# GELU by tanh from the exponential's table, its cubic on VectorE, and other shares of the score tiles

## The chip, the core and the metric

The kernel runs on one core of a Trainium2 chip. A core has TensorE (PE, matrix multiplies into the eight banks of PSUM), ScalarE (ACT, table functions), VectorE (DVE, elementwise work), GpSimd (POOL, a slower elementwise engine that has no part in PSUM here) and SyncE (SP, which issues transfers). They run side by side and wait for one another on semaphores. The metric is device time in microseconds: the median before is 809.54 over four runs (808.48 to 812.94).

## The reference

One transformer block over 2048 tokens of width 640, in bfloat16: a layer norm, attention with 32 query heads of width 20 that share one key and one value head, a residual, a second layer norm, a gated feed-forward with 1536 hidden columns, and a residual.

```python
h  = x + softmax(q @ k.T * 20**-0.5) @ v @ wo        # x normed first; 32 heads, one k and v
h2 = h + (gelu(n @ w_gate) * (n @ w_up)) @ w_down    # n = layernorm(h); gelu(approximate=True)
```

The GELU is the tanh form: 0.5 g (1 + tanh(0.79788 (g + 0.044715 g³))). The attention has 32 x 2048 x 2048 scores, and each of them needs an exponential.

## The kernel before, in words

**Packs.** The scores are made in packs. A unit is 512 query columns for four rows of the array; a pack is one key tile (128 keys) against a unit: four matmuls (L1037, "QK") that fill four PSUM banks, one score tile of 128x512 each. There are 512 packs, 64 for each pair of token tiles. Banks 0 to 5 hold scores, so a new pack needs four of six free: the two spare ones and two that the pack before must have given back. Banks 6 and 7 hold the sums of probabilities times values (L1116, "PV") and all other matmuls.

**Who makes the exponentials.** Of the four tiles of a pack some go to ScalarE, which takes one tile (128x512) or two neighbouring banks at once (128x1024) through `Exp` (L1375), and n go to VectorE, which makes an approximate exponential with a multiply and an add into a 16 bit integer (L1438, "d" below). Each such tile needs two shifted copies, one integer add each; GpSimd makes nearly all of them (L1416, 128x256 int32), VectorE now and then several at once (L1410). So a VectorE tile gives three PV matmuls, a ScalarE tile one. The usual pack has n = 1: one single and one pair for ScalarE, one d for VectorE, two adds for GpSimd.

**The order is planned at build time.** Each engine runs a fixed list. A planner walks simulated time with a cost for each instruction and picks, engine by engine, what to put next; the engines on the chip then follow these lists in order and wait on semaphores. `issue_qk` (L982) chooses n from the ScalarE backlog A and the VectorE load Dv: 0 where Dv is over `TH0`, otherwise 1, and in a burst (A over 3000 ns) 4 or 2. `act_decide` puts a ready ScalarE task ahead of the next exponential.

**The feed-forward.** It goes by batches: seven of two token tiles, and the last two tiles by themselves. Once both normed tiles of a batch stand in `xn2T`, `gate_job` makes the gate product in pieces of 512 columns (two hidden tiles of 128 by 256 tokens), and `up_job` the up product; `down_job` sums 12 matmuls for each half of a token tile. While there are exponentials left, a gate piece is copied from PSUM to `gbuf` by VectorE (L799), and when all six pieces of a batch are there, `gelu` runs `Gelu_apprx_tanh` over them in two ScalarE instructions of 1536 columns (L819). ScalarE holds one set of function tables; `Exp` and this GELU stand in different sets, so a table load (`ACT_TABLE_LOAD`) comes before the two and another after them. Then VectorE multiplies with the up product straight from PSUM (L836). After the last exponential, gates go from PSUM through GELU directly (L801).

Of the kernel before, what the change touches and what calls it, by code (L numbers as in the profile page):

```python
# [178 lines left out]
class _Job:  # L179


    __slots__ = ("name", "prio", "pieces", "bank", "then", "seq", "pos", "gate")

    def __init__(self, name, prio, pieces, then, gate=None):
        self.name = name
        self.prio = prio
        self.pieces = pieces
        self.then = then
        self.bank = None
        self.pos = 0  # L190
        self.gate = gate


def bass_sequential_preLN__grouped_kv_mqa__glu_gated_geglu__prompt_kernel(
# [39 lines left out]
    NQ = 4  # L234
    NXT = 4
    NON = 8

    allocs = []

# [5 lines left out]

    xh = sb("xh", [P, NT, D], BF16)
    xn1T = sb("xn1T", [P, NC_D, S], BF16)
    xn2T = sb("xn2T", [P, NC_D, 1024], BF16)
    wq_pad = sb("wq_pad", [P, NG, NC_D, P], BF16)
    wk_sb = sb("wk_sb", [P, NC_D, Dh], BF16)  # L250
    wk4 = sb("wk4", [P, NC_D, P], BF16)
# [12 lines left out]
    onq = sb("onq", [P, NON, D], BF16)  # L264
    onT = sb("onT", [P, 4, NC_D, P], BF16)
    gbuf = sb("gbuf", [P, NFC, 512], BF16)
    ident = sb("ident", [P, P], BF16)
    halfc = sb("halfc", [P, 4], BF16)
    warm = sb("warm", [P, 4], BF16)
# [40 lines left out]
    def c_dve(n):  # L310
        return n / 0.96 + 67.0

    POOL_ADD = 635.0
    ADD_MIN = 1
    PVF = 99
# [2 lines left out]
    PADD_LEN = 2  # L318
    PRA = 3
    PRD = 3  # L320
    TH0 = 1500.0
    TH2 = 0.0
    PAIR2 = 0
    ADDW = 50.0
    MISCMAX = 1500.0
# [38 lines left out]
    sp_tasks = []  # L364
    state = {"mode": "m", "tab": "exp", "npack": 0, "exps_left": 2048, "misc_ready": False, "kv_left": NT, "qk_left": 512}
    bank_owner = {b: None for b in range(8)}
    slots = {"xt": list(range(NXT)), "q": list(range(NQ)), "onT": list(range(4)), "osb": [0, 1], "rcp": [0, 1]}
    pa_free = [True] * NA
    pd_free = [True] * ND
    pd_next = [0]  # L370
# [23 lines left out]
    def ln_group(ln, tiles, prio, done):  # L394
        n = len(tiles)
        sl = slice(tiles[0], tiles[-1] + 1)
        cnt = [0]
        kk = (ln, tiles[0])

        def after_stats(op):  # L400
            cnt[0] += 1
            if cnt[0] == n:
                dve(lambda e: e.tensor_copy(ln_vb[:, ln, sl], mv[:, ln, sl, 1]), 80,
                    [("mv", ln, t) for t in tiles], [("vb", kk)], prio, c2)

        def c2(op):
            dve(lambda e: e.tensor_scalar_add(ln_veb[:, ln, sl], ln_vb[:, ln, sl], EPS), 80,  # L407
                [("vb", kk)], [("veb", kk)], prio, c3)

        def c3(op):  # L410
            task(("pool",), lambda e: e.tensor_tensor(ln_denb[:, ln, sl], ln_veb[:, ln, sl], halfc[:, 0:n], ALU.pow),  # L411
                 1010, L_POOL, [("veb", kk), "halfc"], [("den", kk)], prio, c4)

        def c4(op):
            dve(lambda e: e.reciprocal(ln_r[:, ln, sl], ln_denb[:, ln, sl]), 90, [("den", kk)], [("lr", kk)],
                prio, c5)

        def c5(op):
            for t in tiles:
                norm(t)  # L420

        def norm(t):
            slot = []

            def gate():
                return bool(slots["xt"])

            def start():
                slot.append(slots["xt"].pop(0))
                return slot[0]  # L430

            def then(op):
                s = slot[0]

                def tdone(op2):
                    slots["xt"].append(s)
                    done(t, op2)

                if ln == 0:
                    o = xn1T[:, :, t * P:(t + 1) * P]  # L440
                    wkeys = [("xn1T", t)]
                else:
                    o = xn2T[:, :, xcol[t]:xcol[t] + P]
                    wkeys = [("xn2T", xcol[t])]
                def free():
                    return ln == 0 or batch_of[t] < 2 or up_left[batch_of[t] - 2] == 0

                if t in (PE_T1 if ln == 0 else PE_T2):
                    tr_job(("tr", ln, t), xn_tmp[:, s, :], ("xt", s), o, wkeys, lambda: slots["xt"].append(s),
                           lambda op2: done(t, op2))  # L450
                    return
                sp_tasks.append(_Task(("sp",), lambda e: e.dma_start_transpose(o, xn_tmp[:, s, :]), 1330, 1700,
                                      [("xt", s)], wkeys, prio, tdone, free))

            keys = [("x", t)] if ln == 0 else [("h", t, 0), ("h", t, 1)]
            tk = _Task(("dve",), None, 310, L_DVE, keys + [("lr", kk)], [], prio, then, gate)

            def bind():
                s = start()
                tk.fn = lambda e: e.tensor_scalar(xn_tmp[:, s, :], xh[:, t, :], mv[:, ln, t, 0:1],  # L460
                                                  ln_r[:, ln, t:t + 1], ALU.subtract, ALU.mult)
                tk.writes = [("xt", s)]

            tk.born = bind
            tasks.append(tk)

        return after_stats
# [13 lines left out]
    xcol = {}  # L481
    for b, tl in enumerate(BATCHES):
        for i, t in enumerate(tl):
            xcol[t] = (b % 2) * 512 + i * P


    def free_bank(b):
# [235 lines left out]
    batch_of = {t: b for b, tl in enumerate(BATCHES) for t in tl}  # L723
    batch_x = [0] * len(BATCHES)
    down_left = [2 * len(tl) for tl in BATCHES]
    gate_left = [NFC] * len(BATCHES)
    up_left = [NFC] * len(BATCHES)
    copied = [[] for _ in BATCHES]

    def x2_done(t, op):  # L730
        b = batch_of[t]
# [40 lines left out]
    def bview(bk, b, k):  # L772
# [2 lines left out]
            return bank(bk, n)  # L775
        return bank(bk, n * k).rearrange("p (k n) -> p k n", k=k)

    def gate_job(b, fc):
        n = len(BATCHES[b]) * P
        k = per_job(b)  # L780
        ks = [x for i in range(k) for x in gkeys(b, fc + i)]

        def then(bk):
            def fin(op):
                free_bank(bk)
                gate_left[b] -= k
                copied[b].append(fc)
                if gate_left[b] == 0:
                    gelu(b)

            def fin2(op):
                free_bank(bk)
                gate_left[b] -= k
                up_job(b, fc)
                if gate_left[b] == 0 and copied[b]:
                    gelu(b)
            o, i = gview(b, fc, k), bview(bk, b, k)
            if state["exps_left"] > 0:
                dve(lambda e: e.tensor_copy(o, i), c_dve(n * k), [("b", bk)], ks, 1.0, fin)  # L799
            else:  # L800
                task(("act",), lambda e: e.activation(o, i, ACT.Gelu_apprx_tanh), ("gelu", c_act(n * k)), L_ACT,  # L801
                     [("b", bk)], ks, 1.0, fin2)
        jobs.append(_Job(("gate", b, fc), 5.0, gu_pieces(wg_sb, b, fc), then, lambda: g_free(b)))

    def gelu(b):
        k = per_job(b)
        fcs = sorted(copied[b])
        runs = []
        n = len(BATCHES[b]) * P
        most = max(k, 1536 // n)  # L810
        for fc in fcs:
            if runs and runs[-1][1] == fc and fc + k - runs[-1][0] <= most:
                runs[-1][1] = fc + k
            else:
                runs.append([fc, fc + k])
        for f0, f1 in runs:
            v = gview(b, f0, f1 - f0)
            ks = [x for fc in range(f0, f1) for x in gkeys(b, fc)]
            task(("act",), (lambda v: lambda e: e.activation(v, v, ACT.Gelu_apprx_tanh))(v),  # L819
                 ("gelu", c_act(n * (f1 - f0))), L_ACT, ks, ks, 1.0,  # L820
                 (lambda f0, f1: lambda op: [up_job(b, fc) for fc in range(f0, f1, k)])(f0, f1))

    def up_job(b, fc):
        n = len(BATCHES[b]) * P
        k = per_job(b)
        ks = [x for i in range(k) for x in gkeys(b, fc + i)]

        def then(bk):
            def fin(op):
                free_bank(bk)  # L830
                up_left[b] -= k
                if up_left[b] == 0:
                    for t in BATCHES[b]:
                        down_job(b, t, 0)
            o, i = gview(b, fc, k), bview(bk, b, k)
            dve(lambda e: e.tensor_tensor(o, i, o, ALU.mult), c_dve(n * k), [("b", bk)] + ks, ks, 1.0, fin)  # L836
        jobs.append(_Job(("up", b, fc), 4.0, gu_pieces(wu_sb, b, fc), then))

    def down_job(b, t, h):
# [142 lines left out]
    def issue_qk(t, u, kt, fb):  # L982
        A = max(act_end() - t, 0.0)
        Dv = dve_load(t)
        if state["tab"] == "gelu" or any(tk.engs[0] == "act" for tk in tasks):
            A += sum(tk.cost[1] for tk in tasks if tk.engs[0] == "act" and isinstance(tk.cost, tuple)) + 1300.0
        nf = pd_free.count(True) - len(dve_q)
        burst = A > 3000.0
        if state["npack"] < 4:
            n = 0  # L990
        elif burst:
            n = 4 if Dv < 2500.0 else 2
        elif Dv > TH0:
            n = 0
        elif Dv < TH2:
            n = 2
        else:
            n = 1
# [303 lines left out]
    def issue_piece(t, jb, pc):  # L1302
        if isinstance(jb, _Start):
# [3 lines left out]
            active.append(jb)  # L1307
            jb.bank = b
            bank_owner[b] = jb.name
            if jb.name[0] == "q":  # L1310
                units[jb.name[1]]["q"] = slots["q"].pop(0)
        b = jb.bank
# [335 lines left out]
```

## Time and profile before

| what | value |
|---|---|
| median of the runs | 809.54 us |
| profiled execution, time and span | 812.94 us and 811.1 us |
| granted TensorE clock, mean | 0.989 |
| ScalarE busy | 761.8 us, 94% of the span |
| TensorE, VectorE, GpSimd busy | 694.7, 571.2, 639.2 us |
| exponentials on ScalarE | 504 pairs, 505 singles; on VectorE 535 tiles |
| table loads | 16, of 1283 ns |
| copies of gates, products with up | 42 of 691 ns (L799), 48 of 683 ns (L836) |
| GpSimd's adds | 1036 of 616 ns |

The profiled execution is 3.4 us above the median, of which 1.8 us lie outside the span. Busy times are unions: neighbouring instructions of an engine overlap in the records, so a mean duration is longer than the step from one to the next. "Idle before" names what ended the idle time in front of a group; an engine that is not the bottleneck idles at no cost.

### The profile page before, as it was taken

The page shows a single profiled execution, that of the slowest core. Times are in us where ns is not written, and L with a number is a line of the kernel's source. Part 1 is how long each engine was busy: PE and PEld are TensorE (multiplying, and loading weights), DVE is VectorE, ACT ScalarE, POOL GpSimd, SP SyncE. Part 2 cuts the span into 40 slices and gives each one's busy share as a digit, 9 for nine tenths or more (in the row PEclk, how much of TensorE's full clock was granted, in tenths as well). Part 3 has the DMA queues.
Part 4 walks back from the last instruction along what each step waited for, and adds up shares of the span by engine and source line. Part 5 has one row for each costly group of instructions (what it writes and reads, how often), then busy time and mean ns, then how long its engine had stood idle before and what let it go on. Part 6 is the DMA issues. An engine that isn't in the chain of part 4 may idle for free.

```text
span 811.1 us, 30789 instructions
## 1 busy us (share of the span) xinstructions
PE 694.7 (86%) x13435; PEld 335.3 (41%) x13435; DVE 571.2 (70%) x1060; ACT 761.8 (94%) x1054; POOL 639.2 (79%) x1096
## 2 busy tenths in 40 slices
PE   4787778889789897889978898898988899888998
PEld 3432223444334443345434443354433444344457
DVE  7865557776687666776677766876668766777854
ACT  3699999999999999999999999999999999999991
POOL 5488788888888888888888888888888778888860
PEclk9899999999999999999999999999999989999999
DMA  7590000100020000000000000100000000000000
GB/s 205 82 336 2 2 1 18 20 2 13 22 21 3 2 19 19 19 2 3 18 19 19 2 11 19 26 3 2 19 18 19 2 2 19 19 18 11 11 19 18
DMA packets 40293, 22.01 MB, mean 27 GB/s; under 512 B 31328, under 2 KB 38880, under 8 KB 40160
## 3 DMA queue, kind: packets, MB, share of 16 engines
q1 hardware_dynamic: 37536, 19.18, 9.8%
q8 instruction: 107, 1.75, 0.9%
q10 hardware_dynamic: 2624, 0.87, 0.5%
q14 instruction: 26, 0.21, 0.1%
HBM read 10.21 MB, written 2.62 MB: 16 GB/s over the span
## 4 chain that ended last, share of the span: by engine, by line
ACT 80%; PE 12%; DVE 4%; DMA 2%; issue 1%; POOL 0%; ACTq 0%
ACT pa L1375 76%; PE ps L1037 3%; PE ps L498 3%; PE ps L1116 3%; PE ps L494 3%; ACT gbuf L819 2%; DVE pd L1438 2%; DMA gbuf<-in_A_wq_dram 1%; ACT L1375 1%; ACT L819 1%; DVE osb L1143 1%; DMA xn1T<-xn_tmp 1%; DVE xn_tmp L460 0%; DVE stats L391 0%; PE ps L1240 0%
## 5 line engine op out<-in xcount | busy, mean ns | idle before, releaser
L1375 ACT ACTIVATE pa<-ps 128x512 bf16<-128x512 f32 (+1 forms) x1009 | 713.2, 953 | 19.3 <-PE ps L1037 19.2
L1416 POOL TENSOR_TENSOR pd<-pd,shifts 128x256 int32<-128x256 int32 x1036 | 615.1, 616 | 130.2 <-DVE pd L1438 119.4
L1438 DVE TENSOR_SCALAR pd<-ps 128x512 uint16<-128x512 f32 x535 | 365.9, 690 | 208.1 <-PE ps L1037 201.8
L1116 PE MATMUL ps<-pd,v_ext 128*32 128x512 bf16 x1605 | 273.1, 385 | 32.7 <-DVE osb L1143 18.3
L1116 PE MATMUL ps<-pa,v_ext 128*32 128x512 bf16 x1513 | 265.4, 387 | 3.8 <-DVE pd L1438 1.7
L1037 PE MATMUL ps<-qT,kT 32*128 32x512 bf16 x2048 | 204.5, 385 | 60.6 <-DVE pd L1438 25.0
L1037 PEld LDWEIGHTS ps<-qT,kT 32*128 32x128 bf16 x2048 | 61.0, 91 | 218.3 <-DVE pd L1438 145.2
L1116 PEld LDWEIGHTS ps<-pd,v_ext 128*32 128x32 bf16 x1605 | 73.6, 95 | 93.1 <-ACT pa L1375 32.7
L1116 PEld LDWEIGHTS ps<-pa,v_ext 128*32 128x32 bf16 x1513 | 70.0, 95 | 48.1 <-issue 33.0
L498 PE MATMUL ps<-xn2T,wu_sb 128*32 128x256 bf16 x1680 | 62.3, 280 | 2.4 <-DVE gbuf L836 2.4
L498 PE MATMUL ps<-wd_sb,gbuf 128*32 128x320 bf16 x1344 | 64.1, 301 | 0.0
L498 PE MATMUL ps<-xn2T,wg_sb 128*32 128x256 bf16 (+1 forms) x1748 | 63.4, 272 | 0.7
L498 PEld LDWEIGHTS ps<-xn2T,wg_sb 128*32 128x32 bf16 x1748 | 42.1, 96 | 19.7 <-issue 12.2
L498 PEld LDWEIGHTS ps<-xn2T,wu_sb 128*32 128x32 bf16 x1680 | 42.4, 98 | 17.9 <-issue 9.5
L498 PE MATMUL ps<-xn1T,wq_pad 128*32 128x256 bf16 (+1 forms) x1440 | 48.0, 266 | 0.0
L498 PEld LDWEIGHTS ps<-wd_sb,gbuf 128*32 128x32 bf16 x1344 | 32.9, 96 | 22.9 <-issue 11.1
L498 PEld LDWEIGHTS ps<-xn1T,wq_pad 128*32 128x32 bf16 x1440 | 32.8, 97 | 14.6 <-issue 10.6
L836 DVE TENSOR_TENSOR gbuf<-ps,gbuf 128x512 bf16<-128x512 f32 x48 | 32.8, 683 | 6.6 <-PE ps L494 6.5
L391 DVE BATCH_NORM_STATS2 stats<-xh 128x6 f32<-128x320 bf16 x64 | 29.9, 483 | 3.5 <-DMA xh<-in_A_x_dram 3.2
L799 DVE CAST gbuf<-ps 128x512 bf16<-128x512 f32 x42 | 29.0, 691 | 0.2 <-PE ps L498 0.2
L498 PE MATMUL ps<-wo_sb,onT 128*32 128x320 bf16 x600 | 27.1, 300 | 0.0
L411 POOL TENSOR_TENSOR ln_denb<-ln_veb,halfc 128x2 bf16<-128x2 bf16 (+1 forms) x18 | 12.5, 695 | 15.7 <-DVE ln_veb L407 14.1
(68 smaller groups left out, 332.0 us busy)
## 6 DMA issues: line engine op xcount, KB each, us to landing
out_dram<-xh SPq DMA_DIRECT2D x16, 160.0 KB, 1.8
xh<-in_A_x_dram SPq DMA_DIRECT2D x3, 640.0 KB, 9.5
wg_sb<-in_B_w_gate_dram SPq DMA_DIRECT2D x1, 1920.0 KB, 10.7
wu_sb<-in_B_w_up_dram SPq DMA_DIRECT2D x1, 1920.0 KB, 15.0
wd_sb<-in_B_w_down_dram SPq DMA_DIRECT2D x1, 1920.0 KB, 19.7
gbuf<-in_A_wq_dram ACTq DMA_DIRECT2D x2, 400.0 KB, 8.7
wo_sb<-in_A_wo_dram SPq DMA_DIRECT2D x1, 800.0 KB, 5.1
xh<-in_A_x_dram SPq DMA_DIRECT2D x2, 160.0 KB, 2.7
```

Source lines behind the costliest of these rows:

```text
L391: dve(lambda e: e.bn_stats(stats[:, ln, t, 6 * h:6 * h + 6], xh[:, t, h * HALF:(h + 1) * HALF]), 356, [key], [("st", ln, t, h)], prio, c)
L411: task(("pool",), lambda e: e.tensor_tensor(ln_denb[:, ln, sl], ln_veb[:, ln, sl], halfc[:, 0:n], ALU.pow), 1010, L_POOL, [("veb", kk), "h ...
L494: return e.matmul(o(b), l, r, start=st, stop=sp)
L498: ins = e.matmul(o(b)[a, :], l[:, a], r, start=st, stop=sp, tile_position=(0, 32 * j))
L799: dve(lambda e: e.tensor_copy(o, i), c_dve(n * k), [("b", bk)], ks, 1.0, fin)
L819: task(("act",), (lambda v: lambda e: e.activation(v, v, ACT.Gelu_apprx_tanh))(v), ("gelu", c_act(n * (f1 - f0))), L_ACT, ks, ks, 1.0, (la ...
L836: dve(lambda e: e.tensor_tensor(o, i, o, ALU.mult), c_dve(n * k), [("b", bk)] + ks, ks, 1.0, fin)
L1037: ins = e.matmul(bank(b), kT4[32 * r:32 * r + 32, kt * P:(kt + 1) * P], qT[32 * r:32 * r + 32, s, :], start=True, stop=True, tile_position ...
L1116: ins = e.matmul(ps[32 * r:32 * r + 32, ab * 512:(ab + 1) * 512], v_ext[:, it["kt"], it["w"], :], it["ap"], start=st, stop=(j in ends), ti ...
L1375: op = plan.commit("act", lambda e: e.activation(dst, src, ACT.Exp, scale=SM_SCALE), cost, L_ACT, [("b", b0 + i) for i in range(n)], [("pa ...
L1416: return e.tensor_tensor(pd32[:, w, h], pd32[:, 0, h], shifts[:, w - 1:w].to_broadcast([P, 256 * k]), ALU.add)
L1438: op = plan.commit("dve", lambda e: e.tensor_scalar(pd[:, 0, s * 512:(s + 1) * 512], bank(b), CH_A, CH_B, ALU.mult, ALU.add), c_dve(512), ...
```

## The change

The table load is done without: a gate piece no longer goes through `Gelu_apprx_tanh` while exponentials are left, but through `Tanh`, which is called from the set that `Exp` uses. Around it VectorE does the rest, on pieces of 512 columns in a new buffer `zt` of six slots, with g halved on the way out of PSUM (o = g/2):

1. G: o = 0.5 x gate (from PSUM, in place of the copy)
2. "1": z = o x o; "2": z = 4 x 0.044715 z + 1; "3": z = z x o (all in SBUF, bfloat16)
3. T on ScalarE: z = tanh(1.59577 z)
4. U: z = (z + 1) x up (from PSUM, in place of the product); F: o = z x o (in SBUF)

A piece goes by itself, as soon as its slot and its gate product are there; nothing waits for a whole batch. The choice of n changes as well: the ScalarE backlog counts all waiting ScalarE tasks, `TH0` rises from 1500 to 2000, and n = 2 is new where the backlog is over 700 ns and the VectorE load under 1000 ns. A pack with n = 2 has two singles for ScalarE and two d. `xn2T` shrinks from 1024 to 768 columns and holds three batches in turn in place of two.

The lists built from it have 568 singles and 456 pairs on ScalarE and 568 d on VectorE, 42 of each of the steps above, two table loads in all, 1051 adds on GpSimd and 85 on VectorE (41 single, 22 double; before 34 in 17 instructions), and 40 matmuls that only keep TensorE busy (L1240) in place of 156. After the last QK of the list stand 96 down matmuls, 10 up matmuls of 256 columns and 109 gate matmuls of 128 columns in the full-array form (before 48, none and 103).

```diff
-    xn2T = sb("xn2T", [P, NC_D, 1024], BF16)
+    xn2T = sb("xn2T", [P, NC_D, 768], BF16)
+    zt = sb("zt", [P, NZ, 512], BF16)
-    TH0 = 1500.0
+    TH0 = 2000.0
+    AH = 700.0
+    THA = 1000.0
+    BURST = 3000.0
...
-                    return ln == 0 or batch_of[t] < 2 or up_left[batch_of[t] - 2] == 0
+                    return ln == 0 or batch_of[t] < 3 or up_left[batch_of[t] - 3] == 0
...
     def gate_job(b, fc):
...
+            def c1(op):
                 free_bank(bk)
+                dve(lambda e: e.tensor_tensor(z, o, o, ALU.mult), c_dve2(w), ks, [("z", s)], 1.0, c2)
+
+            def c2(op):
+                dve(lambda e: e.tensor_scalar(z, z, GA, 1.0, ALU.mult, ALU.add), c_dve4(w), [("z", s)], [("z", s)],
+                    1.0, c3)
+
+            def c3(op):
+                dve(lambda e: e.tensor_tensor(z, z, o, ALU.mult), c_dve2(w), [("z", s)] + ks, [("z", s)], 1.0, c4)
+
+            def c4(op):
+                task(("act",), lambda e: e.activation(zt[:, s, 0:w], zt[:, s, 0:w], ACT.Tanh, scale=2.0 * GC),
+                     c_act(w) + 35.0, L_ACT, [("z", s)], [("z", s)], 1.0, lambda op: up_job(b, fc, s))
             if state["exps_left"] > 0:
-                dve(lambda e: e.tensor_copy(o, i), c_dve(n * k), [("b", bk)], ks, 1.0, fin)
+                dve(lambda e: e.tensor_scalar(o, i, 0.5, None, ALU.mult), c_dve(w), [("b", bk)], ks, 1.0, c1)
...
-    def gelu(b):
-        k = per_job(b)
-        fcs = sorted(copied[b])
...
+            def c1(op):
+                free_bank(bk)
+                dve(lambda e: e.tensor_tensor(o, z, o, ALU.mult), c_dve2(w), [("z", s)] + ks, ks, 1.0, fin)
+            dve(lambda e: e.scalar_tensor_tensor(z, z, 1.0, i, ALU.add, ALU.mult), c_dve(w),
+                [("b", bk), ("z", s)], [("z", s)], 1.0, c1)
...
-        if state["tab"] == "gelu" or any(tk.engs[0] == "act" for tk in tasks):
-            A += sum(tk.cost[1] for tk in tasks if tk.engs[0] == "act" and isinstance(tk.cost, tuple)) + 1300.0
+        A += sum(tk.cost for tk in tasks if tk.engs[0] == "act")
         nf = pd_free.count(True) - len(dve_q)
-        burst = A > 3000.0
+        burst = A > BURST
...
-        elif Dv < TH2:
+        elif Dv < TH2 or (A > AH and Dv < THA):
             n = 2
```

## The prediction, made before the changed kernel ran

> **What bounds the kernel now.** I read the first part of the page and its chain, then the groups of ScalarE by form, then the timeline of ScalarE around a table load, and last VectorE and GpSimd in a quiet stretch.
>
> ```profile
> PE 694.7 (86%) x13435; PEld 335.3 (41%) x13435; DVE 571.2 (70%) x1060; ACT 761.8 (94%) x1054; POOL 639.2 (79%) x1096
> ...
> ACT 80%; PE 12%; DVE 4%; DMA 2%; issue 1%; POOL 0%; ACTq 0%
> ```
>
> ScalarE is busy 94% and holds 80% of the chain. By forms:
>
> ```profile
> L1375 ACT ACTIVATE pa<-ps 128x1024 bf16<-128x1024 f32 x504 | 588.8, 1170 | 5.5 <-PE ps L1037 5.5
> L1375 ACT ACTIVATE pa<-ps 128x512 bf16<-128x512 f32 x505 | 370.8, 737 | 13.8 <-PE ps L1037 13.7
> L819 ACT ACTIVATE gbuf<-gbuf 128x1536 bf16<-128x1536 bf16 x14 | 20.0, 1475 | 0.1
> L819 ACT ACT_TABLE_LOAD x7 | 9.0, 1283 | 0.1
> L1375 ACT ACT_TABLE_LOAD x7 | 9.0, 1283 | 0.0
> ```
>
> The exponentials wait 19.3 us in all. Their records overlap (588.8 and 370.8 sum to far more than the 713.2 of the line's union), so I price them by steps: consecutive ends lie 0.917 us apart for a pair and 0.490 for a single, 1.407 for a usual pack. The timeline of ScalarE at the second batch:
>
> ```profile
> 250.07 9.62 ACT L1375 ACTIVATE pa<-ps 128x1024 bf16<-128x1024 f32 x13
> 259.71 1.28 ACT L819 ACT_TABLE_LOAD   x1
> 261.00 2.86 ACT L819 ACTIVATE gbuf<-gbuf 128x1536 bf16<-128x1536 bf16 x2
> 263.86 1.28 ACT L1375 ACT_TABLE_LOAD   x1
> 265.16 6.71 ACT L1375 ACTIVATE pa<-ps 128x512 bf16<-128x512 f32 x10
> ```
>
> From 259.69 to 265.16 there is no exponential: 5.47 us, seven times. The next view shows the neighbours: VectorE and QK in a quiet stretch.
>
> ```profile
> 343.04 0.69 DVE L1438 TENSOR_SCALAR pd<-ps 128x512 uint16<-128x512 f32 x1
> ...
> 344.02 0.40 PE L1037 MATMUL ps<-qT,kT 32*128 32x512 bf16 x4
> ...
> 344.47 0.69 DVE L1438 TENSOR_SCALAR pd<-ps 128x512 uint16<-128x512 f32 x1 [0.73 <-PE ps L1037]
> 345.13 0.69 DVE L799 CAST gbuf<-ps 128x512 bf16<-128x512 f32 x1
> ...
> 345.24 1.18 POOL L1416 TENSOR_TENSOR pd<-pd,shifts 128x256 int32<-128x256 int32 x2 [0.24 <-DVE pd L1438]
> ```
>
> A pack takes d 0.69 us on VectorE and leaves a hole of 0.73; GpSimd's two adds take 1.18 and leave 0.21 to 0.24. The next QK starts about 0.14 after ScalarE's single and no sooner than 0.06 after d, so ScalarE paces the loop, with some 0.2 to 0.4 us of slack for a late d. Three engines run within a quarter of the pace, and the change takes work from one of them and gives it to the other two.
>
> **The change, part by part** (against the profiled span, 811.1 us).
>
> *ScalarE's own work.* Gone are seven stops of 5.47 us, 38.3, and some 0.7 of overlap lost at their ends: -39.0. Exponentials: 504 x 0.917 + 505 x 0.490 = 709.6 before, 456 x 0.917 + 568 x 0.490 = 696.5 after: -13.1. New are 42 tanh of 512 columns: two GELUs of 1536 take 2.86, so 512 columns can't be under 0.477, and a single exponential of 512 steps by 0.490; from SBUF and small I take 0.53: +22.3 (20.0 to 25). Sum -29.8, if ScalarE is never starved. *The Trainium skill ("ScalarE: Activation LUTs", "What ACT_TABLE_LOAD costs") puts a switch at about 2.66 us with its drain; by that the 14 loads would be worth 37.2 where the trace shows 18.0 and the GELU 0.01 us behind the load, and my sum would be 19 lower; the row decides.*
>
> *Banks behind a pack with n = 2.* There are 60 such packs, 42 near a tanh. There ScalarE does tanh, single, single: 0.53 + 0.98 = 1.51. The QK behind waits for the second d in about half of them and for the first single in many others, and that single now stands behind the tanh. With the ends above, data for the next single come 0.06 us (second d) or 0.23 (first single) after ScalarE could have used them: 0.15 to 0.19 a time, 42 x 0.19 = 8.0; of the other 18, 14 wait for the first d alone and lose nothing: +2. Together +10 (0 to 16).
>
> *VectorE.* A piece adds "1", "2", "3", F. An add of 512 columns alone (L1410) takes 278 ns; at half its rate for two inputs I estimate 410. With overlap that is 0.33, 0.2, 0.33, 0.33, 1.2 us a piece, 50 us in all; 33 more d of 0.6, 20; 51 more adds in fewer, longer instructions, some 10. VectorE goes from 571 to about 650 before any waiting, so it isn't the bound on average. But inside a batch, 39 d and six pieces sum to some 41 us of steps against ScalarE's 45. What it waits for there is GpSimd:
>
> ```profile
> 231.92 0.69 DVE L1438 TENSOR_SCALAR pd<-ps 128x512 uint16<-128x512 f32 x1
> 232.53 0.16 DVE L403 CAST ln_vb<-mv 128x2 bf16<-128x2 f32 x1
> 232.72 0.60 DVE L407 TENSOR_SCALAR ln_veb<-ln_vb 128x2 bf16<-128x2 bf16 x1
> ```
>
> Two columns take 0.60 us when an add of GpSimd has just begun, 0.15 otherwise: a wait of 0.45. Behind it the next d is late. *The Trainium skill ("SBUF — State Buffer", "SBUF: two separate sides") says that VectorE and GpSimd share a port pair that one holds for a whole instruction, and that VectorE instructions with two SBUF inputs ask for it as well; row L407 agrees for the one-input form, and no row here shows two SBUF inputs. By the page all of 1, 2, 3, F and the adds would wait; without it only "2" and the adds.* I bound each of the four by 0 and 0.45 us. "1" starts in GpSimd's hole and "2" comes just when GpSimd has begun again, so d behind them is 0.2 to 0.35 late, which the slack mostly hides. What it doesn't hide is a tanh, in ScalarE's list right behind the pack in which "3" runs: "3" has about 0.35 us to spare, and where both are late ScalarE stands. I take 0.13 a piece, 42 x 0.13 = +5.5 (0 to 0.8 each: 34). Where F and a double add stand between two d (14 times), the next d is up to 0.75 late: 0.3 each, +4 (0 to 8).
>
> *GpSimd.* 1051 adds in place of 1036; in a batch 72 adds of 0.57 are 41 us, and each of 27 VectorE instructions that go between them costs it 0.1 to 0.25: 46 of some 46.5. PV matmuls wait for adds and stand in TensorE's list ahead of the next QK: +2 (0 to 10). Fewer of L1240's matmuls cost nothing that I see: TensorE has 84 of 95 us filled in a period, and its clock reads 1.00.
>
> *The end.* After the last pack the trace is all TensorE:
>
> ```profile
> 787.00:811.10 24.10, 21.32 (x295) 18.68 (x295) 9.67 (x21) 6.76 (x10) 0.56 (x1) 1.00 0.05 15
> ...
> 804.90 3.42 PE L494 MATMUL ps<-wd_sb,gbuf 128*128 128x320 bf16 x24
> ```
>
> 21.3 of 24.1 us, and the rest is the last output. The new list ends with 48 more down matmuls (3.42 / 24 = 0.1425 each: 6.8), ten up of 256 columns (0.11: 1.1) and six gates (0.06: 0.4), which ran under the exponentials before: +8.3 (5 to 8.3; no cover is left).
>
> *Sum.* -29.8 + 10 + 5.5 + 4 + 2 + 8.3 = 0.0. The profiled time is 3.4 above the median of the runs, so on that basis 809.5; the loss terms are skewed upwards, and I say 811. The gain on ScalarE is real, and it is spent on stalls of ScalarE and on a longer end.
>
> **The rivals.**
>
> *Faster: the slack hides it.* If "1", "3" and F don't wait for GpSimd and the batches stay in step, the terms 5.5, 4 and 2 fall to about 1 and the banks' 10 to 6: -29.8 + 7 + 8.3 = -14.5, 795. For it: ScalarE was busy 93.99 of 95 us in a period although each L799 fills VectorE's hole to 0.04 us. Against it: it needs every tanh in time.
>
> *Slower: VectorE's waits for GpSimd decide.* If all four wait 0.3 to 0.45, a piece costs VectorE 1.2 to 1.8 more; less 0.4 of slack that is about 0.8 of ScalarE standing, 42 x 0.8 = 34 in place of 5.5, and the adds 8: -29.8 + 10 + 34 + 8 + 4 + 8.3 = +34, 844. It decides from about 0.3 us lost a piece, where the sum passes +7. For it: 0.60 against 0.15 in L407, and GpSimd 79% busy. Against it: "1" and "3" fall often into GpSimd's hole. Halfway is 826.
>
> *The change doesn't save its loads.* The list has two loads, so 18.0 us go; but a tanh that takes 0.7 would give back 7: 818.
>
> **How the numbers follow.** Terms that about cancel 0.40 (803 to 819), faster 0.27 (788 to 803), waits for GpSimd 0.28 (818 to 844), dear tanh 0.05. Half a per cent, about what this kernel's measurement can tell, is 805.5 and 813.6. Of the first case 0.15 lies below, 0.6 within and 0.25 above: faster 0.27 + 0.06 = 0.33; same 0.25; slower 0.28 + 0.10 + 0.04 = 0.42. The range, with one in ten left out on each side, is 795 to 836; the likeliest case's own is 803 to 819.
>
> **What the profile after would show.** Right: no table load between 30 us and the last pack; tanh of 0.5 to 0.6; ScalarE's busy time near 730 and new idle time on it in front of tanh (released by VectorE's "3") and behind packs with n = 2 (released by QK), some 20 us together; "2" bimodal, 0.28 and 0.7; GpSimd with more records over 650 ns; a stretch behind the last exponential some 8 us longer. Wrong if ScalarE's idle time doesn't grow (faster), if VectorE passes 90% in the batches (slower), or if the last stretch stays at 24 us, which alone is worth 8.

## The result, and the profile after

The changed kernel takes 810.52 us (median of 52 runs, 808.07 to 814.35), the kernel before 809.59 (78 runs, 806.59 to 812.94): a ratio of 1.001, with a 95% interval of 1.0004 to 1.0017. The forecast was 811. Nothing that can be felt has changed in the time, and nearly everything has changed in the profile. Its profiled execution took 809.37 us, span 807.6. First the page of the changed kernel, busy times and chain:

```profile
PE 690.1 (85%) x13193; PEld 332.2 (41%) x13193; DVE 671.5 (83%) x1308; ACT 740.6 (92%) x1082; POOL 662.3 (82%) x1111
...
DVE 39%; PE 37%; ACT 18%; DMA 3%; issue 2%; POOL 0%; ACTq 0%
```

ScalarE held 80% of the chain before and holds 18% now; VectorE went from 4% to 39%. VectorE's busy time alone (83%) doesn't tell this: it is an average, and the chain says that where time is lost VectorE comes last. Next ScalarE's groups by form (columns as before: busy, mean of one, idle before and who ended it):

```profile
L1408 ACT ACTIVATE pa<-ps 128x1024 bf16<-128x1024 f32 x456 | 501.4, 1101 | 2.8 <-PE ps L1068 2.2 <-PE ps L1147 0.6
L1408 ACT ACTIVATE pa<-ps 128x512 bf16<-128x512 f32 x568 | 367.1, 667 | 24.7 <-PE ps L1068 21.6
L827 ACT ACTIVATE zt<-zt 128x512 bf16<-128x512 bf16 x42 | 28.4, 675 | 1.7 <-DVE zt L824 0.9
```

The loads between exponentials are gone, 42 tanh have come, and the exponentials of single tiles wait longer for QK: 21.6 us (L1068), where it was 13.7. What QK waits for stands in the list of waits of TensorE (total us, times, longest), first before, then after:

```profile
PE ps L1037 <- DVE pd L1438: 25.0, 67, 1.2
```

```profile
PE ps L1068 <- DVE pd L1471: 52.0, 116, 1.2
PE ps L1068 <- ACT pa L1408: 12.5, 35, 1.2
```

QK waited 25.0 us in 67 places for a d, and now waits 52.0 in 116. The stretch behind the last exponential, from the table by windows (length, then busy time of PE, PEld, DVE, ACT, POOL, clock, DMA share, GB/s):

```profile
774.65:807.60 32.95, 30.08 (x373) 25.29 (x371) 12.76 (x28) 6.68 (x11) 1.04 (x2) 1.00 0.07 22
```

It was 24.8 us counted the same way. I keep one ledger for all kernels of this document. From the end of the first to the end of the last exponential, ScalarE's *work* is its instructions at their own steps (0.917 a pair, 0.490 a single, 0.51 a tanh, 1.373 a GELU of 1536, 1.29 a load); what its consecutive ends lie further apart is *stall*; with the start (17 us) and the stretch *behind* the last exponential this is the span.

| profiled execution | span | work | stalls | behind |
|---|---|---|---|---|
| before | 811.1 | 746.0 | 23.2 | 24.8 |
| after | 807.6 | 716.5 | 41.3 | 32.9 |
| difference | -3.5 | -29.5 | +18.1 | +8.1 |

So 29.5 us of ScalarE's work went, and 26.2 came back in two places. One profiled execution stands for some microseconds only: by the spans the kernel gained 3.5, by the medians it lost 0.9, because the profiled run of before lay 3.4 above its median and that of after 1.2 below. Terms of that size aren't told apart by a ledger.

Where VectorE loses its time is seen in its groups by form:

```profile
L867 DVE SCALAR_TENSOR_TENSOR zt<-zt,ps 128x512 bf16<-128x512 bf16 x42 | 28.4, 675 | 3.3 <-PE ps L506 3.3
L824 DVE TENSOR_TENSOR zt<-zt,gbuf 128x512 bf16<-128x512 bf16 x42 | 22.7, 541 | 0.0
L820 DVE TENSOR_SCALAR zt<-zt 128x512 bf16<-128x512 bf16 x42 | 22.7, 540 | 1.0
L817 DVE TENSOR_TENSOR zt<-gbuf 128x512 bf16<-128x512 bf16 x42 | 21.8, 519 | 0.0
L866 DVE TENSOR_TENSOR gbuf<-zt,gbuf 128x512 bf16<-128x512 bf16 x42 | 21.3, 507 | 0.0
...
L1443 DVE TENSOR_SCALAR pd<-pd 128x1024 uint16<-128x1024 uint16 x22 | 17.2, 782 | 0.0
```

"2" (L820) takes 275 to 283 ns in 4 cases, 319 in one and 460 to 697 in 37. These 37 start within an add of GpSimd that still has over 0.25 us to go, and all end 0.15 to 0.16 us behind its end. The add has begun 0.25 to 0.49 us before the instruction ahead of "2" ended (that is "1" in 29 of the 37), and most of these adds take 0.72 to 0.82 us where the mean before was 0.62: GpSimd waits for VectorE as well. "1", "3" and F (L817, L824, L866) take 407 to 417 in most cases when no add is under way, and up to 906, 817 and 829 when one is. U (L867) with one input from PSUM is never longer: 29 of 42 started within an add, 17 of them with over 0.25 us of it to go, and none of the 42 took over 0.69. So VectorE does wait with two SBUF inputs, which no row of before could show. *The Trainium skill ("SBUF — State Buffer", "SBUF: two separate sides") has this rule, against a GpSimd instruction that reads SBUF; L817, L824 and L866 agree with it.* And one place, in the timeline of the changed kernel:

```profile
259.31 1.36 POOL L1449 TENSOR_TENSOR pd<-pd,shifts 128x256 int32<-128x256 int32 x2
...
259.49 0.72 DVE L866 TENSOR_TENSOR gbuf<-zt,gbuf 128x512 bf16<-128x512 bf16 x1
...
259.73 0.40 PE L1068 MATMUL ps<-qT,kT 32*128 32x512 bf16 x4
260.13 0.83 DVE L1443 TENSOR_SCALAR pd<-pd 128x1024 uint16<-128x1024 uint16 x1
260.88 0.68 DVE L1471 TENSOR_SCALAR pd<-ps 128x512 uint16<-128x512 f32 x1
...
261.70 0.40 PE L1068 MATMUL ps<-qT,kT 32*128 32x512 bf16 x4 [0.59 <-DVE pd L1471]
262.15 1.51 ACT L1408 ACTIVATE pa<-ps 128x512 bf16<-128x512 f32 x2 [0.36 <-PE ps L1068]
```

F waits for the add that began at 259.31 (0.72 in place of 0.41), the double add behind it waits for the next one (0.83 in place of 0.41). The d of the pack at 259.73 therefore starts at 260.88 and not near 260.2, the next QK waits 0.59 for it, and ScalarE stands. The two QK lie 1.97 us apart.

### The profile page after: what moved, and what is told of

It is laid out like the page before. It is cut to its first block, busy times and chain, and to the rows that moved or that the text cites. A ratio compares the mean times of both kernels' runs of the same rounds, so it can differ in the third digit from the quotient of the medians.

```text
span 807.6 us, 30618 instructions
## 1 busy us (share of the span) xinstructions
PE 690.1 (85%) x13193; PEld 332.2 (41%) x13193; DVE 671.5 (83%) x1308; ACT 740.6 (92%) x1082; POOL 662.3 (82%) x1111
## 4 chain that ended last, share of the span: by engine, by line
DVE 39%; PE 37%; ACT 18%; DMA 3%; issue 2%; POOL 0%; ACTq 0%
DVE pd L1471 21%; ACT pa L1408 18%; PE ps L510 13%; PE ps L1068 12%; PE ps L1147 8%; PE ps L506 4%; DVE zt L820 2%; DVE gbuf L830 2%; DVE zt L817 2%; DVE pd L1443 2%; DVE osb L1174 2%; DVE zt L824 1%; DVE zt L867 1%; DMA gbuf<-in_A_wq_dram 1%; DVE xn_tmp L472 1%
## 5 line engine op out<-in xcount | busy, mean ns | idle before, releaser
L1449 POOL TENSOR_TENSOR pd<-pd,shifts 128x256 int32<-128x256 int32 x1051 | 638.4, 632 | 100.0 <-DVE pd L1471 89.7
L1471 DVE TENSOR_SCALAR pd<-ps 128x512 uint16<-128x512 f32 x568 | 384.5, 686 | 102.4 <-PE ps L1068 97.1
L1068 PE MATMUL ps<-qT,kT 32*128 32x512 bf16 x2048 | 204.3, 386 | 80.0 <-DVE pd L1471 52.0
L1147 PE MATMUL ps<-pa,v_ext 128*32 128x512 bf16 x1480 | 260.4, 388 | 3.7 <-DVE pd L1471 1.6
L1068 PEld LDWEIGHTS ps<-qT,kT 32*128 32x128 bf16 x2048 | 59.1, 91 | 237.6 <-DVE pd L1471 152.1
L510 PE MATMUL ps<-wd_sb,gbuf 128*32 128x320 bf16 x1152 | 54.3, 301 | 0.0
L510 PEld LDWEIGHTS ps<-xn2T,wu_sb 128*32 128x32 bf16 x1640 | 38.7, 96 | 17.6 <-issue 9.3
L510 PEld LDWEIGHTS ps<-wd_sb,gbuf 128*32 128x32 bf16 x1152 | 28.4, 96 | 19.5 <-issue 9.7
L867 DVE SCALAR_TENSOR_TENSOR zt<-zt,ps 128x512 bf16<-128x512 bf16 x42 | 28.4, 675 | 3.3 <-PE ps L506 3.3
L1443 DVE TENSOR_SCALAR pd<-pd 128x512 uint16<-128x512 uint16 (+1 forms) x63 | 30.1, 483 | 0.0
L827 ACT ACTIVATE zt<-zt 128x512 bf16<-128x512 bf16 x42 | 28.4, 675 | 1.7 <-DVE zt L824 0.9
L830 DVE TENSOR_SCALAR gbuf<-ps 128x512 bf16<-128x512 f32 x42 | 28.6, 682 | 0.1
```

The lines of the kernel that those rows point to most:

```text
L510: ins = e.matmul(o(b)[a, :], l[:, a], r, start=st, stop=sp, tile_position=(0, 32 * j))
L827: task(("act",), lambda e: e.activation(zt[:, s, 0:w], zt[:, s, 0:w], ACT.Tanh, scale=2.0 * GC), c_act(w) + 35.0, L_ACT, [("z", s)], [("z" ...
L830: dve(lambda e: e.tensor_scalar(o, i, 0.5, None, ALU.mult), c_dve(w), [("b", bk)], ks, 1.0, c1)
L867: dve(lambda e: e.scalar_tensor_tensor(z, z, 1.0, i, ALU.add, ALU.mult), c_dve(w), [("b", bk), ("z", s)], [("z", s)], 1.0, c1)
L1068: ins = e.matmul(bank(b), kT4[32 * r:32 * r + 32, kt * P:(kt + 1) * P], qT[32 * r:32 * r + 32, s, :], start=True, stop=True, tile_position ...
L1147: ins = e.matmul(ps[32 * r:32 * r + 32, ab * 512:(ab + 1) * 512], v_ext[:, it["kt"], it["w"], :], it["ap"], start=st, stop=(j in ends), ti ...
```

## The experiments

My theory went into the runs as the prediction had it: new stalls from banks behind packs with n = 2 and from VectorE's waits for GpSimd, plus the longer end. The rivals were that one of them is the whole, and that ScalarE still sets the pace. Each ratio is to the kernel before on the same chip; its medians there were 810.0 to 810.5.

**GpSimd out of the way.** Lists, waits and order stay; only the size of its adds is cut:

```diff
-            h = slice(s0 * 256, (s0 + k) * 256)
+            m = 1 if (w, s0) in seen else 256
+            h = slice(s0 * 256, s0 * 256 + m)
```

> The changed kernel with its lists, waits and order as they are, but each of GpSimd's adds writes one column in place of 256, from the second use of a slot on (the weights 0.79 and 0.64 of most VectorE tiles are left out). GpSimd is then hardly ever in VectorE's way and its adds come early. Theory (ScalarE's new stalls come in part from VectorE waiting for GpSimd, in part from the banks, and the tail has nothing to do with it): the terms 5.5 and 4 for VectorE and 2 for PV go, and some of the old stalls, so 796 to 801 in place of 810.5, with ScalarE's stalls before its last exponential at about 28 in place of 41 us. Rival 1 (VectorE's waits for GpSimd are the whole of the new stalls): 788 to 792, stalls near 20. Rival 2 (they are hidden, the banks behind packs with two VectorE tiles are all): 808 to 811.

> The same cut of GpSimd's adds in the kernel before (same weights left out), as the yardstick for the run of the changed kernel. Theory: before the change few VectorE instructions wait for GpSimd, so only a little of the 23 us of stalls goes: 804 to 808 in place of 809.5, and the changed kernel gains at least 5 us more by the cut. Rival 2 (GpSimd is no matter for the change): both kernels gain the same, whatever it is.

Measured: the changed kernel 795.26 us (ratio 0.9806, 0.9786 to 0.9826), stalls 29.8; the kernel before 811.29 (1.0014, 1.0002 to 1.0027), stalls 21.4. The first is just below theory's range, the second above it (804 to 808). The cut is worth 15 us to the changed kernel and nothing to the one before. QK's wait for d falls back nearly to what it was before the change (25.0 us):

```profile
PE ps L1068 <- DVE pd L1472: 27.7, 67, 1.2
```

VectorE's groups in the changed kernel with small adds:

```profile
L866 DVE TENSOR_TENSOR gbuf<-zt,gbuf 128x512 bf16<-128x512 bf16 x42 | 17.4, 415 | 0.0
L817 DVE TENSOR_TENSOR zt<-gbuf 128x512 bf16<-128x512 bf16 x42 | 17.4, 415 | 0.0
L824 DVE TENSOR_TENSOR zt<-zt,gbuf 128x512 bf16<-128x512 bf16 x42 | 17.4, 414 | 0.0
L820 DVE TENSOR_SCALAR zt<-zt 128x512 bf16<-128x512 bf16 x42 | 12.2, 291 | 1.0
...
L1443 DVE TENSOR_SCALAR pd<-pd 128x1024 uint16<-128x1024 uint16 x22 | 9.1, 414 | 0.0
```

Against the rows above, the waits are 92, 104, 127 and 249 ns for F, "1", "3" and "2", 0.57 us a piece, and 0.37 a double add: 24 and 8 us of VectorE's time. The same place of the list as in the timeline above:

```profile
258.16 0.42 DVE L866 TENSOR_TENSOR gbuf<-zt,gbuf 128x512 bf16<-128x512 bf16 x1
...
258.41 0.40 PE L1068 MATMUL ps<-qT,kT 32*128 32x512 bf16 x4
258.49 0.42 DVE L1443 TENSOR_SCALAR pd<-pd 128x1024 uint16<-128x1024 uint16 x1
258.85 0.69 DVE L1472 TENSOR_SCALAR pd<-ps 128x512 uint16<-128x512 f32 x1
...
259.72 0.40 PE L1068 MATMUL ps<-qT,kT 32*128 32x512 bf16 x4
```

The two QK are 1.31 us apart in place of 1.97, and ScalarE doesn't stop.

**The tanh made small.**

```diff
-                task(("act",), lambda e: e.activation(zt[:, s, 0:w], zt[:, s, 0:w], ACT.Tanh, scale=2.0 * GC),
+                task(("act",), lambda e: e.activation(zt[:, s, 0:2], zt[:, s, 0:2], ACT.Tanh, scale=2.0 * GC),
```

> The changed kernel with lists, waits and order as they are, but each of the 42 tanh works on 2 of its 512 columns (the tanh of the rest is left out). ScalarE's own work falls by 42 x 0.44 = 18.5 us (estimate: step of 0.51, less 0.07 for what is left of a step when the 512 columns go, by 0.490 for 512 and 0.917 for 1024). Theory (behind a pack with two VectorE tiles the next QK waits in about half of the cases for the second VectorE tile and in half for the single behind the tanh): only about half comes through, 798 to 803 in place of 810.5. Rival 1 (ScalarE still sets the pace, its own work comes through whole): 790 to 793. Rival 2 (VectorE sets the pace around every piece): 807 to 811.

Measured: 810.09 us (1.0001, 0.9987 to 1.0015), that is, nothing. A small tanh has a step of 0.18, so 13.5 us of ScalarE's work went, and the stalls rose by 12.5, from 41.3 to 53.8. ScalarE's groups of this run:

```profile
L1408 ACT ACTIVATE pa<-ps 128x512 bf16<-128x512 f32 x568 | 365.2, 659 | 38.2 <-PE ps L1068 34.8 <-PE ps L1147 0.7
L827 ACT ACTIVATE zt<-zt 128x2 bf16<-128x2 bf16 x42 | 10.4, 248 | 2.3 <-DVE zt L824 1.5
```

Nearly every microsecond saved on a tanh turns into waiting for QK (idle in front of singles 24.7 to 38.2). The place from above, which has no tanh of its own, is as it was: QK at 258.90 and 260.88. QK's wait for exponentials of ScalarE, 12.5 us, didn't fall either (13.5). So it isn't the single behind the tanh that holds the QK up; half of my bank mechanism is refuted.

**The cubic and the last product made small**, and both cuts together. In the diff `z2` and `o2` are two columns, as are `zo` and `oo` from a slot's second use on:

```diff
-                dve(lambda e: e.tensor_tensor(z, o, o, ALU.mult), c_dve2(w), ks, [("z", s)], 1.0, c2)
+                dve(lambda e: e.tensor_tensor(zo, oo, oo, ALU.mult), c_dve2(w), ks, [("z", s)], 1.0, c2)
-                dve(lambda e: e.tensor_scalar(z, z, GA, 1.0, ALU.mult, ALU.add), c_dve4(w), [("z", s)], [("z", s)],
+                dve(lambda e: e.tensor_scalar(z2, z2, GA, 1.0, ALU.mult, ALU.add), c_dve4(w), [("z", s)], [("z", s)],
...
-                dve(lambda e: e.tensor_tensor(o, z, o, ALU.mult), c_dve2(w), [("z", s)] + ks, ks, 1.0, fin)
+                dve(lambda e: e.tensor_tensor(o2, z2, o2, ALU.mult), c_dve2(w), [("z", s)] + ks, ks, 1.0, fin)
```

> The changed kernel with lists, waits and order as they are, but the two squares and products, the scaling between them and the last product of each piece ('1', '2', '3' and F) work on 2 columns, '1' in full at the first use of a slot (so the cubic and the last product are left out for nearly all columns). VectorE loses about 1.5 us a piece, and hardly anything of the four can wait for GpSimd for long. Theory: the terms 5.5 (tanh waiting for '3') and most of the 4 (F between two VectorE tiles) go, the banks' 10 and the tail's 8.3 stay: 801 to 805 in place of 810.5. Rival 1 (VectorE sets the pace around every piece): below 795. Rival 2 (all four lie in VectorE's holes): 808 to 811.

> The changed kernel with its lists and waits as they are, with both cuts at once: GpSimd's adds of one column, and '1', '2', '3' and F of 2 columns (the weights of most VectorE tiles and the cubic with the last product of nearly all columns are left out). Alone the first took 15.2 us off and the second 12.7. Theory (VectorE is late behind the pieces both by what its five instructions take and by what it waits for GpSimd; the second cut leaves the waits of the 2-column instructions in place): the cuts add up for the most part, 787 to 791 with ScalarE's stalls at 21 to 24 us, near those of the kernel without the sharing rule (20.8). Rival (it is one and the same wait of VectorE for GpSimd that both take away): 794 to 796, stalls of 28 to 30.

Measured: 797.85 us (0.9849, 0.9833 to 0.9865), stalls 31.2, where theory said 801 to 805; with small adds as well 794.55 (0.9808, 0.9777 to 0.9839), no better than the small adds alone (795.26). Taking VectorE's instructions away and taking GpSimd out of their way remove the same late d. Whether the instructions cost anything beyond their waits stays open: the medians say no, the one profile of both cuts (span 791.2, stalls 24.4) hints at a few microseconds.

**The sharing rule alone**, away from the changed kernel and into the one before:

```diff
-    AH = 700.0
+    AH = 1e9
```

```diff
-    TH0 = 1500.0
+    TH0 = 2000.0
-        elif Dv < TH2:
+        elif Dv < TH2 or (A > 700.0 and Dv < 1000.0):
```

> The changed kernel without the new rule that gives VectorE two of four tiles when ScalarE has work waiting; the lists are planned anew: 516 pairs and 513 singles in place of 456 and 576, no pack with two VectorE tiles, 60 down matmuls at the end in place of 96 and no up matmuls. Theory (such a pack saves ScalarE 0.43 us and costs some 0.17 us in banks): ScalarE's own work grows by 28 us, the banks' 10 go, the end gets 7 shorter, VectorE's waits lose some 3: 818 in place of 810.5 (815 to 822). Rival 1 (the rule loses as much in banks and at the end as it saves): 808 to 812. Rival 2 (the rule's packs are worth their full 0.43 each): 828 or more.

> The kernel before with the new sharing rule and the threshold of 2000 alone, with GELU from its own table as it was; planned anew: 482 pairs and 526 singles in place of 504 and 505, 29 packs with two VectorE tiles in place of 6, the same seven stops, 48 down matmuls at the end as before. Theory: ScalarE's own work falls by 22 x 0.917 - 21 x 0.490 = 9.9 us, 23 more packs cost 0.17 to 0.19 each in banks, 4: 804 in place of 809.5 (801 to 806). Rival 1 (such a pack is worth nothing): 809 to 811. Rival 2 (its full worth): 799 to 800.

Measured: 808.17 us without the rule (0.998, 0.9966 to 0.9994), and 815.12 for the kernel before with it (1.0058, 1.0039 to 1.0076). Both miss my theory; the first is the rival by which the rule loses as much as it saves (808 to 812), the second misses every case I had named. The ledger:

| profiled execution | span | work | stalls | behind |
|---|---|---|---|---|
| after | 807.6 | 716.5 | 41.3 | 32.9 |
| after, no rule | 806.5 | 743.1 | 20.8 | 25.9 |
| before | 811.1 | 746.0 | 23.2 | 24.8 |
| before, with the rule | 813.6 | 736.1 | 34.7 | 25.1 |

The 60 shared packs save 26.6 us of ScalarE's work, 0.44 each as foreseen, and come with 20.5 us of stalls, 0.34 each with all that VectorE waits for (banks alone were 0.17), and 7.0 us at the end. In the kernel before 23 more such packs save the 9.9 that I worked out, and the stalls grow by 11.5. But this run can't price a pack, because its clock is another: 0.960 to 0.968 in its four runs, 0.993 on average in those of the kernel before beside them. The windows of the second GELU stop and of the stretch behind it (columns as above, the clock third from the end), first before, then with the rule:

```profile
259.70:265.70 6.00, 5.14 (x102) 2.70 (x98) 5.70 (x10) 5.97 (x6) 5.79 (x11) 1.00 0.01 3
263.20:270.00 6.80, 5.00 (x92) 2.26 (x88) 4.72 (x10) 6.78 (x10) 5.30 (x9) 1.00 0.00 0
```

```profile
261.70:267.70 6.00, 2.31 (x46) 1.08 (x41) 6.00 (x10) 5.97 (x6) 4.54 (x8) 0.79 0.02 4
265.20:272.00 6.80, 4.83 (x56) 1.56 (x52) 4.15 (x8) 5.67 (x8) 1.25 (x2) 0.50 0.00 1
```

With the rule the clock is halved for 58.0 us in all up to the last exponential (before: 17.1), at or just behind the end of every one of the seven stops among others. In the 7.5 us behind each stop ScalarE stalls 0.87 to 1.98 us; in the kernel before it is 0.11 or 0.12 behind the five stops at full clock and 1.2 behind each of the two where the clock was halved. Counted over the run, stalls in these stretches or up to 1.5 us behind them are 20.9 us (before 9.5), and outside them 13.8 (before 13.7): the 11.5 go with the clock. TensorE is busy 2.3 us of the 6 from the start of the stop in place of 5.1, and the list has 44 of L1240's matmuls in place of 156; that the clock falls for this reason fits, but no run tests it. What a shared pack costs the kernel before at full clock stays open. The changed kernel and the one without the rule had 17.1 and 13.7 us of half clock, so the 60 packs' price doesn't rest on it.

The profile without the rule looks like before again:

```profile
ACT 80%; PE 10%; DVE 7%; DMA 2%; issue 1%; SPq 0%
```

And of its waits of TensorE the one that had grown:

```profile
PE ps L1068 <- DVE pd L1471: 18.8, 56, 0.8
```

ScalarE has its 80% of the chain back, and QK waits 18.8 us for d in place of 52.0. This run also prices the GELU half of the change: against before, 2.9 us less work in all. By the ledger's steps the seven stops were 37.3 and 43 tanh are 21.9; the rest went with VectorE's tiles: it took 535 before and takes 508 here, and 12 more pairs and 3 more singles on ScalarE are 12.5 us. (The counts of singles in the expectations of kernels with tanh hold five to eight other instructions as well, mostly the five or six GELUs behind the last exponential.)

**One instruction fewer.** From here on the question is what can be got back. The cubic with two instructions:

```diff
-                dve(lambda e: e.tensor_scalar(z, z, GA, 1.0, ALU.mult, ALU.add), c_dve4(w), [("z", s)], [("z", s)],
-                    1.0, c3)
-                dve(lambda e: e.tensor_tensor(z, z, o, ALU.mult), c_dve2(w), [("z", s)] + ks, [("z", s)], 1.0, c4)
+                dve(lambda e: e.scalar_tensor_tensor(z, z, 1.0 / GA, o, ALU.add, ALU.mult), c_dve(w),
+                    [("z", s)] + ks, [("z", s)], 1.0, c4)
...
-                task(("act",), lambda e: e.activation(zt[:, s, 0:w], zt[:, s, 0:w], ACT.Tanh, scale=2.0 * GC),
+                task(("act",), lambda e: e.activation(zt[:, s, 0:w], zt[:, s, 0:w], ACT.Tanh, scale=2.0 * GC * GA),
```

> The changed kernel with two instructions for the cubic in place of three: the square as it is, then (z + 1/GA) * o in one scalar_tensor_tensor, with GA moved into the scale of the tanh; planned anew (48 packs with two VectorE tiles in place of 60, 468 pairs and 561 singles, 96 down matmuls at the end, no up matmuls). Theory (VectorE's waits for GpSimd make up 5.5 to 10 us): one instruction fewer that asks for GpSimd's port saves 2 to 4, 12 fewer packs cost ScalarE 12 x (0.43 - 0.19) = 3, the end is 1.8 shorter: 807 to 810. Rival 1 (the new instruction runs at a full 0.6 us and waits as well, VectorE sets the pace): 813 or more. Rival 2 (VectorE doesn't matter): 811 to 813.

> The folded cubic without the sharing rule, planned anew: 516 pairs and 514 singles, no pack with two VectorE tiles, 52 down matmuls at the end in place of 60. Theory (VectorE's waits for GpSimd cost time only where the rule has given VectorE a second tile; without it VectorE has time to spare and folding saves nothing): 806 to 809, as the unfolded kernel without the rule (808.2), and ScalarE's stalls at 20 to 21 us. Rival (a wait saved on VectorE is worth the same wherever it stands): 802 to 805, and so no slower than the folded kernel with the rule (804.2).

Measured: 804.17 us (0.993, 0.9913 to 0.9947), better than expected (807 to 810) and faster than both kernels; without the sharing rule 809.1 (0.9986, 0.9972 to 1.0001), at the upper edge of what theory had. VectorE's groups of the folded kernel with the rule:

```profile
L820 DVE SCALAR_TENSOR_TENSOR zt<-zt,gbuf 128x512 bf16<-128x512 bf16 x43 | 30.6, 711 | 0.0
...
L863 DVE TENSOR_TENSOR gbuf<-zt,gbuf 128x512 bf16<-128x512 bf16 x43 | 20.1, 467 | 0.0
L817 DVE TENSOR_TENSOR zt<-gbuf 128x512 bf16<-128x512 bf16 x43 | 18.9, 439 | 0.4
```

The new instruction takes 0.68 us by itself, as long as "2" and "3" free of waits (0.28 and 0.41). What it saves is the meeting: it starts with an add of GpSimd well under way (over 0.25 us to go) in 5 of 43 cases, "2" did in 37 of 42, and the sum of the records of "1" to "3" and F goes from 2.11 to 1.62 us a piece. The ledger says where that went: work 722.1, stalls 31.4, behind 31.1. Of the stalls, 9.7 more than folded without the rule (21.7) go on 48 shared packs, 0.20 each. So folding pays 6.4 us by the medians with the rule and nothing without it (808.17 before folding). The lists were planned anew both times: a part of the 6.4 is that 48 packs are shared in place of 60, and no run takes it apart.

**The end made shorter.** The same batches, with a piece's instructions on VectorE ahead of the rest:

```diff
-                dve(lambda e: e.tensor_tensor(z, o, o, ALU.mult), c_dve2(w), ks, [("z", s)], 1.0, c2)
+                dve(lambda e: e.tensor_tensor(z, o, o, ALU.mult), c_dve2(w), ks, [("z", s)], 0.3, c2)
...
-                [("b", bk), ("z", s)], [("z", s)], 1.0, c1)
+                [("b", bk), ("z", s)], [("z", s)], 0.5, c1)
```

> The changed kernel with the priority of a piece's instructions on VectorE moved from 1.0 to 0.3 (the halving of the gate, '1', '2', '3') and 0.5 (the product with up), so that batches end earlier; planned anew: 451 pairs and 579 singles, 65 packs with two VectorE tiles in place of 60, and at the end 48 down matmuls in place of 96, no up of batch 6 in place of 10, 8 gates more. Theory (the tail is worth what its matmuls take, and stalls go with the number of shared packs at 0.34 us each): tail -7.5, ScalarE's own work -3.1, 5 more shared packs +1.7: 801.5 in place of 810.5 (799 to 804). Rival (pulling the pieces ahead of the VectorE tiles makes those later and starves ScalarE by as much): 808 or more.

> The kernel with the folded cubic (804.2) with the priority of a piece's instructions on VectorE at 0.5 in place of 1.0; 47 shared packs in place of 48, 469 pairs and 561 singles, 49 down matmuls at the end in place of 96. Theory: as in the run above the tail's matmuls alone, -5.4: 799 (797 to 801). Rival (VectorE tiles come later and take it back): 803 or more.

Measured: 812.96 us (1.0035, 1.002 to 1.005) and, folded, 811.36 (1.0008, 0.9991 to 1.0024): the rival both times. The chain of the first:

```profile
DVE 48%; PE 38%; ACT 9%; DMA 3%; issue 2%; POOL 0%; ACTq 0%
```

Its waits of ScalarE:

```profile
ACT pa L1408 <- PE ps L1068: 31.9, 70, 3.9
...
ACT zt L827 <- DVE zt L824: 3.5, 15, 0.6
```

The end did get 7.6 shorter (32.9 to 25.3), and the stalls grew by 11.7 (41.3 to 53.0); folded, 5.5 shorter against 15.4 (of which 5.3 in or just behind stretches of half clock, 27.3 us in place of 17.1). The end is long because VectorE does the tiles first; this order doesn't take it off for free.

**The rule held back.** The folded kernel, the rule only where VectorE has little ahead:

```diff
-    THA = 1000.0
+    THA = 500.0
```

> The folded cubic with the sharing rule held to moments in which VectorE has under 500 ns of work ahead (THA at 500 in place of 1000): 40 shared packs in place of 48, 476 pairs and 553 singles in place of 468 and 561, 69 down matmuls at the end in place of 96. Theory: ScalarE's own work +3.4, 8 shared packs fewer at 0.22 us of stall each -1.8, the end -3.9: 802 in place of 804.2 (800 to 804). Rival (as in the two runs with the pieces first, work that leaves the end comes back as ScalarE's stalls): 805 or more.

Measured: 801.70 us (0.9894, 0.9871 to 0.9917), the fastest of the kernels that leave nothing out, 8 us below both; its interval just touches that of the folded kernel (0.9913 to 0.9947). Ledger: work 726.0, stalls 29.8, behind 27.6; against the folded kernel +3.9, -1.6 and -3.5, as expected within half a microsecond each. The spans (801.0 and 802.1) show less of the gain than the medians.

## Why the prediction was right, point by point

The number was right, and so was the sentence it stood on: the gain on ScalarE is real and is spent on stalls and a longer end. That the sum came out within a microsecond is luck in part: the stalls arise in another way than described, the range was wide (795 to 836), and of the three outcomes "same" had the lowest chance, 0.25. The steps came out as follows.

- *ScalarE's own work*, -29.8 predicted, -29.5 by the ledger. Two of its parts, the stops (37.3 for 39.0) and the tanh (20.9 for 22.3), are off by about as much and cancel. Without the rule 41 of 43 tanh step by 0.507 to 0.512, where I took 0.53; the rival of the dear tanh had 0.7.
- *The tail*, +8.3 predicted, +8.1 measured.
- *The stalls*, +21.5 as the sum of four terms (10, 5.5, 4 and 2), +18.1 measured, of which 2.4 less in the first 40 us (9.1 to 6.7) was not foreseen. By size even the division is near: cutting GpSimd's adds takes off 11.5 us of stalls (15 us of the time by the medians), where 5.5, 4 and 2 make 11.5, and it leaves 29.8 against 21.4 in the kernel before with the same cut, 8.4 where the banks had 10. How they arise is not as I had it.
- *The late d* is the step that failed: d "late, which the slack mostly hides", and a tanh that nothing hides. It is the other way round. ScalarE idles 1.7 us in all in front of tanh, while QK's waits for d went from 25.0 to 52.0 us and fall to 27.7 with GpSimd's adds cut. The waits of "1", "2", "3", F and the double adds reach ScalarE through d and QK.
- *The banks' 10* stood half on another thing that isn't so, the QK that waits "for the first single in many others, and that single now stands behind the tanh". With tanh next to nothing 0.4 us of 13.5 came back by the medians. The term's own two delays, 0.06 and 0.23, also average 0.145 and not 0.19, which makes 6 for the 42 packs and not 8. What the 8.4 left after cutting the adds consist of, no run tells: none cuts tanh and adds together.
- *GpSimd to PV*, +2: not seen; PV's weight loads wait 23.4 us for its adds where they waited 26.7.
- *The slower rival* named the right mechanism at too high a price. It had 1.2 to 1.8 us of waits a piece; the rows give 0.57. It had put all of that less 0.4 on ScalarE.
- *The faster rival* is refuted for this kernel: VectorE's slack doesn't hide the waits where the rule shares tiles. Without the rule it does (20.8 us of stalls, fewer than before).
- Of what I wanted to see, "2" is bimodal (0.28 and 0.59, I had said 0.7), GpSimd's records over 650 ns went from 25 to 190, and ScalarE's new idle time stands in front of singles behind QK, far more than in front of tanh (1.7 us). ScalarE is busy 740.6 us, where I had 730.

What I hadn't thought of is how the two halves of the change work against each other: the rule hands VectorE a second tile when ScalarE has work waiting, a tanh in most cases, which is when VectorE has just done three instructions for it and will soon do two more. That folding, and so fewer waits, saves time with the rule and not without it is measured; this reason for it is how I read the lists. By the medians the GELU half alone is 1.8 us faster than before and the rule takes 2.3 back.

## What to carry to other kernels

When work leaves the engine that sets the pace, price what the relief costs the engine that gets it at the very moment of the transfer, not by its busy share: a rule that fires on the backlog of one engine should look at what that same event has just put before the other. An instruction that starts each time just as another engine has taken something both need is worth more than its own length, and fusing it away can pay even where the fused one is as long as the two together. A long end behind a planned schedule isn't free to remove: pulling its work forward can cost more stalls than it saves. And look at the granted clock of every run before reading a difference: one planned list here had it halved for 58 us, and its stalls went with that.

## What the runs showed of the hardware

Two things I hadn't expected. A `tensor_tensor` on 512 columns of bfloat16 in SBUF takes 0.41 us and up to 0.91 with an add of GpSimd under way; `scalar_tensor_tensor` on the same operands takes 0.68, and up to 1.09. And small instructions don't escape: with "2" cut to two columns it still took 0.48 us on average and up to 0.62 with GpSimd's adds at full size, so for that instruction the wait, not the length, is the price. In the changed kernel an instruction that finds an add of GpSimd with over 0.25 us to go ends a fixed time behind it, 0.15 to 0.16 us for "2" and 0.28 to 0.29 for "1", "3" and F, in 77 of 78 cases.
